# Attention, second block of each head pair: a vector-engine queue in another order

## The chip, the cores and the metric

The kernel runs on one core of one Trainium2 chip. The metric is the device time of one execution in microseconds (us). The engines are named as in the profile: PE is TensorE's matmul, DVE is VectorE, ACT is ScalarE, POOL is GpSimd, SP is SyncE, which here only issues DMAs.

## The reference

Three layers run one after the other. The change is in the first, attention in which a query sees the keys of its own hash bucket only (2 batches, 8 heads, 768 positions, 64 features a head):

```python
mask = q_bucket[:, :, :, None] == k_bucket[:, :, None, :]
scores = scale * np.matmul(q, k.transpose(0, 1, 3, 2))
scores = np.where(mask, scores, -1000000000.0)
scores = scores - np.max(scores, axis=-1, keepdims=True)
attn = np.exp(scores)
attn = attn / (np.sum(attn, axis=-1, keepdims=True) + 1e-09)
return np.matmul(attn, v).astype(np.float32)
```

Behind it stand a feed-forward layer (1536 tokens, 512 to 1024 to 512 features, with a softmax and a layer norm between) and a routed layer of 8 experts. The weights of the feed-forward layer arrive as float64 and are turned into float32 by bit operations, in small steps that the attention's program strews between its own.

## The kernel before, in words

Attention works on pairs of heads: j runs from 0 to 7, and the two heads of a pair lie side by side on the 128 partitions. The 768 queries of a pair are taken in two halves, i = 0 and i = 1. One pass for (j, i) is called a block here, written (j, 0) or (j, 1). In a block c runs over six chunks of 128 keys. `score` (L242) multiplies keys by queries on PE into one of three PSUM buffers called `ps`, ACT takes the exponential into SBUF (`pt`, L252), and POOL adds the exponentials up (`acc`, L256 for two chunks, L258 for the running sum). `rowmax` (L218) computes scores for a later block, into the same three buffers in turn, and DVE reduces them to the row maximum (L225, called a reduce below). So each `ps` buffer comes free either when ACT has taken the exponential or when DVE has reduced, and PE takes the buffers strictly in turn.

Work of the block before is put in at c = 1. In a block (j, 1) it is:

- `av(j, 0)` (L267): exponentials times values on PE, into `x`;
- `evac` (L272): DVE copies a column of `x` into `vb` (L276, the bias column), and ACT copies `x` to `xr` with that bias (L279);
- `sums`, which calls `total` (L281): PE sums the exponentials over keys into `pm` (L287), and DVE adds a small constant into `rb` (L293). In the last pair `direct` (L319) stands in its place: it goes on with a reciprocal (L324) and a product (L325) on DVE;
- `norm(j - 1)` (L313): DVE multiplies `xr` of the pair before by its quotients `rd`, which came back by DMA (L317, 128x768). The quotients come from `recip` (L302) in block (j, 0).

Each block also takes one unit of the float64 weights (`Weights.steps`, L414): `ops` is a list of five or six steps, and `some(m)` emits the next m of them. The steps are an ACT copy (L450), three DVE bit operations (L451, L454, L457, called first, second and last float64 step here), then for the first eight units an ACT cast (L466) and a POOL subtraction (L467), for the last eight an ACT scaling (L462). In a block (j, 1) the ACT copy stands at c = 0, the three DVE steps at c = 1, and the fourth of all (ACT) at c = 3. Units of the first kind fall to j = 0 to 3, of the second kind to j = 4 to 7.

There is no scheduler. Each engine executes its instructions in the order in which this Python code emits them, so the order of the calls in `run` is the order of every queue:

```python
self.av(j, 0, half[0])
some(3)
self.evac(j, 0)
(self.sums if nx else self.direct)(j, 0)
if j:
    self.norm(j - 1)
```

In the last block (7, 1) there are no row maxima left to compute, and `av(7, 1)` is split: its first three chunks are emitted at c = 4, the others behind the loop.

Of the kernel before, what the change touches and what calls it, by code (L numbers as in the profile page):

```python
# [118 lines left out]
class Attention:  # L119
# [207 lines left out]
    def run(self, n, extra, fills):  # L327
        self.last = (n - 1, 1)
        scan = [(j, i, c, kh) for j in range(n) for i in range(2) for c in range(3) for kh in range(2)]

        def scans(m):
            for x in scan[:m]:
                self.rowmax(*x)
            del scan[:m]

        next(extra)
        self.hash(0)
        self.tables()
        self.mask(0)
        scans(NC)  # L340
        self.submax(0, 0)
        scans(3)
        half = [tuple(range(NC)), (0, 1, 2), (3, 4, 5)]
        for j in range(n):
            nx = j + 1 < n
            for i in range(2):
                ops = next(extra, [])

                def some(m):
                    for f in ops[:m]:  # L350
                        f()
                    del ops[:m]

                for c in range(NC):
                    self.score(j, i, c)
                    scans(((2, 1, 0, 1, 1, 1), (2, 1, 1, 1, 1, 0))[i][c])
                    if c == 1:
                        if nx or i == 0:
                            self.submax(*((j, 1) if i == 0 else (j + 1, 0)))
                        if i == 0:  # L360
                            some(1)
                            if nx:
                                self.turn(j + 1)
                            some(1)
                            if j:
                                self.av(j - 1, 1, half[0])
                            if nx:
                                self.hash(j + 1)
                            if j:
                                self.evac(j - 1, 1)  # L370
                                self.sums(j - 1, 1)
                            some(1)
                            if nx:
                                self.mask(j + 1)
                                if j:
                                    self.load(j + 1, "v")
                            if j + 2 < n:
                                self.load(j + 2, "qk")
                        else:
                            self.av(j, 0, half[0])  # L380
                            some(3)
                            self.evac(j, 0)
                            (self.sums if nx else self.direct)(j, 0)
                            if j:
                                self.norm(j - 1)
                            if fills:
                                fills.pop(0)()
                    elif c != 2:
                        some(1)
                    if j and (i, c) == (0, 4):  # L390
                        self.recip(j - 1)
                    if c == 4 and (j, i) == self.last:
                        self.av(j, 1, half[1])
                some(9)
        self.av(n - 1, 1, half[2])
        self.evac(n - 1, 1)
        self.direct(n - 1, 1)
        for ops in extra:
            for f in ops:
                f()  # L400
# [821 lines left out]
```

## Time and profile before

| what | us |
|---|---|
| median of 3 runs (lowest, highest) | 637.66 (636.53, 638.45) |
| profiled execution, its own time | 638.34 |
| span of the profiled execution | 636.6 |
| PE busy in the span | 592.2 (93%) |
| DVE busy | 426.4 (67%) |
| ACT busy | 279.7 (44%) |
| POOL busy | 324.1 (51%) |

The span reaches from the first to the last instruction of the profile; the execution's own time is 1.74 us longer. The attention stage ends at some 262 us of the span. In the rows below each timeline line holds the start, the duration, the engine, the source line, the operation, out<-in with shapes, how many instructions are merged, and in brackets the idle time ahead of it on its engine with what ended that. Consecutive DVE instructions overlap a little in the records: the next starts up to 0.1 us before the end of the last.

### The profile page before, as it was taken

The numbers are of one execution on the slowest core, as the hardware profiler recorded it, in microseconds if no ns is written. First come the engines' busy times: TensorE is split into PE (matmuls) and PEld (weight loads), VectorE is DVE, ScalarE is ACT, GpSimd is POOL, SyncE is SP. The second block draws the span as 40 slices with busy tenths as digits, with TensorE's granted clock in tenths as the row PEclk, the third lists the DMA queues.
The fourth block names the chain that finished last, engine by engine and source line by source line (L and its number), as shares of the span: only waits on it lengthen the run. The fifth ranks groups of instructions, "written<-read, shape, count | busy, mean of one in ns | idle before, by whom it ended". The sixth has DMA issues, their size and how long they took to land.

```text
span 636.6 us, 10142 instructions
## 1 busy us (share of the span) xinstructions
PE 592.2 (93%) x3906; PEld 461.7 (73%) x3906; DVE 426.4 (67%) x800; ACT 279.7 (44%) x465; POOL 324.1 (51%) x262
## 2 busy tenths in 40 slices
PE   4889989899999998959999999989999999999994
PEld 2656556665666665648888888877998898899893
DVE  4868888787868786586767877764656636636630
ACT  3255454556575644343224233232734634544520
POOL 1148676666657577471100004031869659659641
PEclk9789999899999999989999999998999999999998
DMA  7134435362726241700000003016574674687200
GB/s 170 46 83 103 133 102 146 89 165 70 199 66 173 86 129 30 261 1 0 1 1 1 1 2 83 1 68 230 185 241 152 253 264 127 254 292 253 69 20 33
DMA packets 70165, 72.95 MB, mean 115 GB/s; under 512 B 36187, under 2 KB 47195, under 8 KB 70110
## 3 DMA queue, kind: packets, MB, share of 16 engines
q1 hardware_dynamic: 63838, 57.13, 30.1%
q10 hardware_dynamic: 4032, 8.79, 4.4%
q0 software_dynamic: 2240, 6.31, 2.9%
q8 instruction: 32, 0.52, 0.4%
q14 instruction: 23, 0.19, 0.1%
HBM read 58.39 MB, written 14.78 MB: 115 GB/s over the span
## 4 chain that ended last, share of the span: by engine, by line
PE 78%; DVE 12%; issue 3%; ACT 3%; DMA 2%; POOL 1%; SPq 0%; POOLq 0%; ACTq 0%; DVEq 0%
PE g L1004 14%; PE ps L214 14%; PE o L1026 14%; PE h L547 10%; PE y L547 10%; PE x L267 6%; DVE m L225 3%; DVE w L454 2%; PE ps L165 2%; PE t L610 2%; PE pm L287 1%; ACT pt L252 1%; PE x L971 1%; PE ps L200 1%; DVE w L457 1%
## 5 line engine op out<-in xcount | busy, mean ns | idle before, releaser
L256 POOL TENSOR_TENSOR acc<-pt,pt 128x768 f32<-128x768 f32 x48 | 92.3, 1923 | 98.6 <-ACT pt L252 98.6
L944 POOL TENSOR_TENSOR wl<-ws,wh 128x512 fp32r<-128x512 f32 x75 | 107.2, 1463 | 53.4 <-ACT wh L942 53.0
L225 DVE TENSOR_REDUCE m<-ps 128x2 f32<-128x768 f32 x96 | 89.1, 953 | 35.4 <-PE ps L214 34.6
L252 ACT ACTIVATE pt<-ps 128x768 f32<-128x768 f32 x96 | 76.2, 816 | 36.7 <-PE ps L214 36.1
L942 ACT CAST wh<-ws 128x512 fp32r<-128x512 f32 x128 | 70.3, 618 | 5.2 <-POOL wl L944 2.6
L267 PE MATMUL x<-pt,v 128*64 128x385 f32 x384 | 65.8, 491 | 0.0
L944 DVE TENSOR_TENSOR wl<-ws,wh 128x512 fp32r<-128x512 f32 x53 | 57.8, 1124 | 10.3 <-ACT wh L942 8.6
L1010 DVE SCALAR_TENSOR_TENSOR hl<-g,hh 128x512 fp32r<-128x512 f32 x32 | 22.1, 691 | 59.8 <-ACT hh L1009 49.3
L523 POOL TENSOR_TENSOR xl<-xT,xh 128x512 fp32r<-128x512 f32 x12 | 15.6, 1304 | 83.2 <-PE h L547 43.6
L258 POOL TENSOR_TENSOR acc<-acc 128x768 f32<-128x768 f32 x30 | 56.0, 1868 | 2.4
L1009 ACT ACTIVATE hh<-g 128x512 fp32r<-128x512 f32 x32 | 19.2, 599 | 81.4 <-PE g L1004 58.0
L547 PE MATMUL h<-wi,xh 128*128 128x512 f32 x192 | 51.2, 410 | 0.0
L1026 PE MATMUL o<-wh,hh 128*128 128x512 f32 x128 | 51.1, 399 | 0.0
L1026 PE MATMUL o<-wh,hl 128*128 128x512 f32 x128 | 50.5, 394 | 0.0
L1026 PE MATMUL o<-wl,hh 128*128 128x512 f32 x128 | 50.5, 394 | 0.0
L267 PEld LDWEIGHTS x<-pt,v 128*64 128x64 f32 x384 | 26.1, 137 | 31.7 <-issue 30.9
L214 PE MATMUL ps<-Hk,Hq 64*128 64x384 f32 x192 | 41.4, 421 | 7.3 <-ACT pt L252 7.2
L214 PE MATMUL ps<-Hq,Hk 64*128 64x384 f32 x192 | 39.5, 407 | 3.5 <-ACT pt L252 1.7
L547 PE MATMUL y<-wo,lh 128*128 128x512 f32 x176 | 42.6, 394 | 0.0
L547 PEld LDWEIGHTS h<-wi,xh 128*128 128x128 f32 x192 | 35.9, 194 | 8.0 <-ACT xh L538 0.6
L1004 PE MATMUL g<-xh,wh 128*128 128x256 f32 x256 | 41.3, 283 | 0.3 <-ACT xh L973 0.3
L1004 PE MATMUL g<-xl,wh 128*128 128x256 f32 x256 | 41.2, 282 | 0.0
(221 smaller groups left out, 1234.9 us busy)
## 6 DMA issues: line engine op xcount, KB each, us to landing
ws<-in_moe_w_dram SPq DMA_DIRECT2D x32, 1024.0 KB
scratch<-zero SPq DMA_DIRECT2D x7, 1030.0 KB
r<-scratch SPq DMA_DIRECT2D x16, 257.5 KB
raw<-in_moe_w_in_dram ACTq DMA_DIRECT2D x8, 512.0 KB
raw<-in_moe_w_out_dram ACTq DMA_DIRECT2D x8, 512.0 KB
q<-in_q_dram SPq DMA_DIRECT2D x16, 192.0 KB
v<-in_v_dram SPq DMA_DIRECT2D x16, 192.0 KB
k<-in_k_dram SPq DMA_DIRECT2D x14, 192.0 KB
```

Source lines behind the costliest of these rows:

```text
L214: self.nc.tensor.matmul(ps[:, h], w[r], x[r], start=(n == 0), stop=(n == len(jobs) - 1), tile_position=(D * h, 0))
L225: nc.vector.tensor_reduce(out=st["m", i][:, c, :, kh], in_=ps, axis=AX.X, op=ALU.max, negate=True)
L252: nc.scalar.activation(out=pt[:, :, 0:HW], in_=ps, func=AF.Exp, scale=0.125)
L256: nc.gpsimd.tensor_tensor(out=acc, in0=st["pt", i, c - 1][:, :, 0:HW], in1=pt[:, :, 0:HW], op=ALU.add)
L258: nc.gpsimd.tensor_tensor(out=acc, in0=parts.pop(), in1=acc, op=ALU.add)
L267: nc.tensor.matmul(st["x", i][D * h:D * h + D, 0:HW + 1], st["v"][:, h, c, :], st["pt", i, c][:, h, 0:HW + 1], start=(c == 0), stop=(c == ...
L547: nc.tensor.matmul(ps, a[:, k, :], w[j](k), start=(n == 0), stop=(n == len(jobs) - 1))
L942: nc.scalar.copy(hi[:, k, :], t[:, k, :])
L944: eng.tensor_tensor(out=lo[:, k, :], in0=t[:, k, :], in1=hi[:, k, :].bitcast(F32), op=ALU.subtract)
L1004: nc.tensor.matmul(ps[:, a, :], w[:, k, f * P:(f + 1) * P], x[:, k, :], start=(n == 0), stop=(n == 11))
L1010: nc.vector.scalar_tensor_tensor(out=hl[:, 2 * g:2 * g + 2, :], in0=ps, scalar=0.0, in1=hi.bitcast(F32), op0=ALU.max, op1=ALU.subtract)
L1026: nc.tensor.matmul(st["o"][t], h[:, f, t * P:(t + 1) * P], w[:, f % 4, :], start=(f == 0 and n == 0), stop=(f == 7 and n == 2),)
```

## The change

Only the branch for i = 1 changes. At c = 1 two of the three DVE float64 steps are emitted, then the bias column and the sums, and then the third step. The product `norm` leaves c = 1 and goes to c = 2, where no float64 step stands, behind that chunk's `score` and `rowmax`.

```diff
                         else:
                             self.av(j, 0, half[0])
-                            some(3)
+                            some(2)
                             self.evac(j, 0)
                             (self.sums if nx else self.direct)(j, 0)
-                            if j:
-                                self.norm(j - 1)
+                            some(1)
                             if fills:
                                 fills.pop(0)()
                     elif c != 2:
                         some(1)
+                    elif j and i:
+                        self.norm(j - 1)
```

The queues of PE, ACT, POOL and SP keep their order; only DVE's changes. On DVE, in block (2, 1), from the second float64 step on, before:

```order
L454 SCALAR_TENSOR_TENSOR w<-raw,w 128x512
L457 SCALAR_TENSOR_TENSOR w<-raw,w 128x512
L276 COPY vb<-x 128x1
L293 TENSOR_SCALAR rb<-pm 128x384
L317 TENSOR_TENSOR xT<-xr,rd 128x768
L225 TENSOR_REDUCE m<-ps 128x2 x6
```

and with the change (lines behind the edit are one number higher):

```order
L455 SCALAR_TENSOR_TENSOR w<-raw,w 128x512
L276 COPY vb<-x 128x1
L293 TENSOR_SCALAR rb<-pm 128x384
L458 SCALAR_TENSOR_TENSOR w<-raw,w 128x512
L225 TENSOR_REDUCE m<-ps 128x2
L317 TENSOR_TENSOR xT<-xr,rd 128x768
L225 TENSOR_REDUCE m<-ps 128x2 x5
```

The last float64 step (L457, now L458) has moved behind `vb` and `rb`, and the product L317 behind the first reduce. The blocks of the other pairs from 1 to 6 change in the same way; block (0, 1) has no product. In the last block (7, 1) DVE has, before:

```order
L454 SCALAR_TENSOR_TENSOR w<-raw,w 128x512
L457 SCALAR_TENSOR_TENSOR wo_70<-raw,w 128x512
L276 COPY vb<-x 128x1
L293 TENSOR_SCALAR rb<-pm 128x384
L324 RECIPROCAL rb<-rb 128x384
L325 TENSOR_TENSOR xT<-xr,rb 128x384
L317 TENSOR_TENSOR xT<-xr,rd 128x768
```

and with the change:

```order
L455 SCALAR_TENSOR_TENSOR w<-raw,w 128x512
L276 COPY vb<-x 128x1
L293 TENSOR_SCALAR rb<-pm 128x384
L324 RECIPROCAL rb<-rb 128x384
L325 TENSOR_TENSOR xT<-xr,rb 128x384
L458 SCALAR_TENSOR_TENSOR wo_70<-raw,w 128x512
L317 TENSOR_TENSOR xT<-xr,rd 128x768
```

Here the last float64 step moves behind the reciprocal and the product of `direct` as well.

## Rows read from the trace of the kernel before

**Rows 1.** Waits, whole span: who waited for whom, us in total, times, longest.

```profile
ACT xr L279 <- DVE vb L276: 51.3, 10, 6.3
```

**Rows 2.** Timeline of PE in block (3, 1), from the sums to the last score.

```profile
139.99 0.86 PE L287 MATMUL pm<-acc,ones 128*64 128x384 f32 x4
...
141.41 0.34 PE L214 MATMUL ps<-Fq,Fk 64*128 64x384 f32 x2
...
142.46 0.34 PE L214 MATMUL ps<-Fq,Fk 64*128 64x384 f32 x2
144.16 0.51 PE L214 MATMUL ps<-Hk,Hq 64*128 64x384 f32 x2 [1.36 <-ACT pt L252]
...
145.04 0.44 PE L214 MATMUL ps<-Hq,Hk 64*128 64x384 f32 x2 [0.19 <-DVE m L225]
...
146.20 0.34 PE L214 MATMUL ps<-Hq,Hk 64*128 64x384 f32 x2
```

**Rows 3.** Timeline of ACT and POOL in block (3, 1).

```profile
142.83 0.58 ACT L279 ACTIVATE xr<-x,vb 128x384 f32<-128x384 f32 x1 [6.20 <-DVE vb L276]
143.31 1.51 ACT L252 ACTIVATE pt<-ps 128x768 f32<-128x768 f32 x2
...
139.90 2.28 POOL L256 TENSOR_TENSOR acc<-pt,pt 128x768 f32<-128x768 f32 x1
144.89 1.84 POOL L256 TENSOR_TENSOR acc<-pt,pt 128x768 f32<-128x768 f32 x1 [2.72 <-ACT pt L252]
```

**Rows 4.** Timeline of DVE in block (3, 1).

```profile
138.30 2.18 DVE L454 SCALAR_TENSOR_TENSOR w<-raw,w 128x512 int32<-128x512 int32 x1
140.52 2.21 DVE L457 SCALAR_TENSOR_TENSOR w<-raw,w 128x512 int32<-128x512 int32 x1
142.65 0.14 DVE L276 COPY vb<-x 128x1 f32<-128x1 f32 x1
...
143.18 0.94 DVE L317 TENSOR_TENSOR xT<-xr,rd 128x768 f32<-128x768 f32 x1
144.04 1.81 DVE L225 TENSOR_REDUCE m<-ps 128x2 f32<-128x768 f32 x2
```

**Rows 5.** Timeline of POOL, DVE and PE in block (4, 1).

```profile
168.26 2.08 POOL L256 TENSOR_TENSOR acc<-pt,pt 128x768 f32<-128x768 f32 x1
168.69 2.20 DVE L454 SCALAR_TENSOR_TENSOR w<-raw,w 128x512 int32<-128x512 int32 x1
...
170.93 0.69 DVE L457 SCALAR_TENSOR_TENSOR wo<-raw,w 128x512 int32<-128x512 int32 x1
...
172.18 0.34 PE L214 MATMUL ps<-Fq,Fk 64*128 64x384 f32 x2
...
175.09 0.34 PE L214 MATMUL ps<-Hq,Hk 64*128 64x384 f32 x2
```

**Rows 6.** Timeline of DVE and PE in block (0, 1).

```profile
49.83 2.24 DVE L457 SCALAR_TENSOR_TENSOR w<-raw,w 128x512 int32<-128x512 int32 x1
...
51.77 0.34 PE L214 MATMUL ps<-Fq,Fk 64*128 64x384 f32 x2
...
55.24 0.44 PE L214 MATMUL ps<-Hq,Hk 64*128 64x384 f32 x2
```

**Rows 7.** Timeline of ACT, DVE and PE in the last block (7, 1).

```profile
255.47 0.72 ACT L462 ACTIVATE wo<-wo,g 128x512 f32<-128x512 f32 x1
...
256.38 1.52 DVE L325 TENSOR_TENSOR xT<-xr,rb 128x384 f32<-128x384 f32 x1
...
258.29 2.16 PE L267 MATMUL x<-pt,v 128*64 128x385 f32 x12
258.46 0.81 ACT L252 ACTIVATE pt<-ps 128x768 f32<-128x768 f32 x1 [1.56 <-PE ps L214]
```

**Rows 8.** Stretches: us, busy time of PE, PEld, DVE, ACT, POOL, granted clock, DMA.

```profile
110.00:113.90 3.90, 2.35 (x24) 1.76 (x20) 3.90 (x6) 2.19 (x4) 1.18 (x2) 1.00 0.85 230
113.90:117.40 3.50, 3.47 (x22) 3.48 (x24) 1.79 (x2) 1.11 (x2) 3.42 (x2) 0.54 0.23 48
```

## The prediction

> **What bounds the kernel now.** I read the waits first, then the timelines of PE, ACT, POOL and DVE for one block (j, 1), each against the others. PE sets the end of the attention stage, and its gaps in a block (j, 1) are made elsewhere. ACT's longest wait in this stage is that for the bias column `vb`: 51.3 us in ten waits [rows 1]. In block (3, 1) PE has done the score of chunk 3 at 142.80 (142.46 + 0.34) and then stands 1.36 us until 144.16, because the buffer that it wants next still holds chunk 2, whose score was done at 141.75 (141.41 + 0.34) [rows 2]. ACT takes that exponential only at 143.31, since `xr` is ahead of it in ACT's queue, and `xr` waited 6.20 us for `vb` [rows 3]. `vb` runs at 142.65, behind the last float64 step [rows 4]. A second wait follows: the score of chunk 4, at 145.04, waits for a reduce [rows 2], and that reduce stands at 144.04 behind `vb`, `rb` and the product L317 [rows 4]. So DVE's queue sets the pace for some 3 us in each block (j, 1), and the order of the queue is what changes.
>
> **How long the last float64 step takes.** It lasts 2.21 us in block (3, 1) [rows 4] and 0.69 in block (4, 1) [rows 5]. The difference is POOL. POOL's add ends at 142.18 (139.90 + 2.28) [rows 3], and the step ends at 142.73, 0.55 later [rows 4]. In block (4, 1) an add ends at 170.34 and the second float64 step at 170.89, again 0.55 later [rows 5]. A DVE operation with both inputs in SBUF waits there for the POOL instruction that is running and then runs nearly whole. The Trainium skill's page "SBUF — State Buffer", section "SBUF: two separate sides", says this as a rule: an exclusive lock on a shared port pair, held for the whole instruction by whichever began first. By proportional sharing a step would stretch with its overlap; by the rule an early start gains nothing, and these two ends agree with the rule.
>
> **Blocks (1, 1) to (3, 1).** I work out (3, 1) and take the other two as its repeats.
> - `vb` comes behind the second step, which ends at 140.48 (138.30 + 2.18) [rows 4]; that is 2.2 us earlier. `xr` then runs to about 141.2, and exponential 2 from 141.85, 0.1 after its score, for 0.81 [rows 7]. PE goes on at 142.76 in place of 144.16.
> - `rb` waits for PE's sums, done at 140.85 [rows 2], and with it the last step comes up at 141.4. POOL is in its add until 142.18, so the step still ends at 142.73. Moving it gains nothing in itself; it only lets `vb` and `rb` pass.
> - The first reduce now follows at 142.65, where `vb` stood, instead of 144.04: 0.53 for `vb` and `rb` and 0.86 for the product lie no longer ahead of it [rows 4]. PE's score of chunk 4 can start at 143.70 in place of 145.04.
> - The product comes next, at 143.52 (a reduce takes its place in the queue for 0.87), and the second reduce at 144.38, done at 145.33. PE would want that buffer at 144.76 (143.70 + 1.06, one chunk's score and row maximum: 142.46 − 141.41 [rows 2]) and gets it at 145.42. So a new wait of 0.66 us appears, for the reduce behind the product. Before, the last score started at 146.20 [rows 2]. The gain is 0.78 us a block, 2.34 in three.
>
> The product has two SBUF inputs too. POOL's next add follows exponential 3: score 3 ends at 142.80, the exponential at 143.71, the add starts at 143.78 (before, 0.07 after the exponential's end [rows 3]). The product at 143.52 is 0.26 us ahead of it. I take it that the product goes first and POOL waits; this is the narrowest step of the sum. If it goes first, POOL's add is still done earlier than before.
>
> **Blocks (4, 1) to (6, 1).** The second step ends at 170.89, POOL is idle from 170.34, so the last step takes 0.69 in either order [rows 5]. `vb` and `rb` end at 171.4, the step holds DVE until 171.94, the reduce, the product and the second reduce start at 171.94, 172.81 and 173.67, and the last is done at 174.63. The last score starts at 174.72 in place of 175.09 [rows 5]: 0.37 a block, 1.1 in three. POOL's add comes 0.98 after the end of score 3 (172.52), at 173.50, 0.7 behind the product's start.
>
> **Block (0, 1)** has no product. The last step ends at 52.07 as before [rows 6]; the reduce starts at 51.99 and ends at 52.93; the score of chunk 4 starts at 53.03 and the last at 54.09, in place of 55.24 [rows 6]: 1.15 us.
>
> **Block (7, 1) loses.** The last step now stands behind the product of `direct`, which ends at 257.90 (256.38 + 1.52), so it ends at 258.50. ACT's scaling L462 needs it. It ran at 255.47 and now runs at 258.5, and exponentials 4 and 5 stand behind it in ACT's queue. Exponential 5 started at 258.46 [rows 7]; with 0.62 for the scaling's place in the queue (0.72 less an overlap of 0.1) and 0.70 for exponential 4's (1.51 − 0.81 [rows 3, 7]) it now starts at 259.8 and ends at 260.6. PE's second part of `av`, which ended at 260.45 [rows 7], needs 0.7 for the last chunk after that (a third of 2.16) and ends at 261.4, and the feed-forward layer starts that much later: 1.0 us lost. `norm(6)` itself is wanted much later.
>
> **Sum.** 1.15 + 2.34 + 1.1 − 1.0 = 3.6 us gained. Against the profiled execution of 638.34 that is 634.7. That execution lies 0.7 above the median of 637.66; from the median it is **634.1**. The bounds of the one unknown place: the product costs 0.86 where it stands, or, behind a POOL add, 2.9 (below).
>
> **The rivals.**
> - *POOL goes first (slower).* If the add takes the port before the product in (1, 1) to (3, 1), the product waits until 145.62 (143.78 + 1.84) and needs 0.8 more, to 146.42; the second reduce ends at 147.29, and the last score starts at 147.4, 1.2 later than before. Three blocks lose 3.5, the others still gain 1.15 + 1.1 − 1.0: +2.3, so 640.0 from the median. The product of `direct` shows such a wait: 128x384 in 1.52 us [rows 7]. It decides at a lead of 0.26 us, which must shrink to nothing; three blocks have the same lead, so they would go together. The Trainium skill's page "Perfetto Trace Analysis", section "GPSIMD Engine Instruction", speaks for this rival: recorded spans of that engine are to be treated as unreliable. By that the add's true start could be before the recorded one; no run here shows it. Chance 0.14.
> - *The gain is given back.* PE runs ahead, but POOL's chain of adds starts only some 0.5 earlier and the next blocks wait for something that did not move. Against it: the sums of (j, 1) are taken a whole stretch of PE work later. Then only (0, 1) and (7, 1) count, 1.15 − 1.0, about 637.5. Chance 0.20.
> - *The clock comes back too.* Right behind the gap of block (2, 1) the granted clock is 0.54 for 3.50 us, after 2.35 of 3.90 us busy [rows 8]; that is mostly 1.2 instead of 2.4 GHz and costs 1.6 us (3.50 × 0.46). PE's waits in such a block shrink and split. If the clock stays at 2.4 GHz there, the time is 632.5. Chance 0.15.
>
> **How the numbers follow.** The forecast itself gets 0.51. What a measurement can tell from no change is about 0.3%, 1.9 us, so the line for faster is 635.8. Forecast and clock rival lie below it: 0.66. The second rival is the same: 0.20. The first is slower: 0.14. The range leaves out the first rival alone and takes in the clock rival and the second: 631.8 to 637.8.
>
> **What would show it.** Right: `xr` waits about 2 us less for `vb` in blocks (0, 1) to (3, 1); PE's 1.36 us wait for the exponential is gone and one of about 0.7 for the reduce behind the product is there; the last step still ends 0.55 behind POOL's add in (0, 1) to (3, 1); the product lasts 0.94; in (7, 1) L462 waits for the float64 step and the feed-forward layer starts 1.0 late. Wrong: a product of 2 us or more, blocks after (j, 1) that take back the gain, or a last block that loses nothing.

## The result, and the profile after

| | before | changed |
|---|---|---|
| median of seven runs each, us | 637.66 | 632.62 |
| ratio of the times | 1 | 0.9911, 95% interval 0.989 to 0.9932 |
| profiled execution, its own time | 638.34 | 631.40 |
| its span | 636.6 | 629.7 |

By the medians the change makes the kernel 5.0 us faster, by the ratio 5.7 (4.3 to 7.0). One of the seven runs of the changed kernel was slow, 1975.9 us, and is left out of the ratio. Forecast were 3.6, with 5.2 for the case that the clock comes back too. Where the time came from is read block by block. I take the start of PE's sums of (j, 0) (L287, in the middle of block (j, 1)) and the next transposes (L165, at the start of work for the next pair) from the timelines of PE. Pair 6 has no transposes behind it, so sums to sums stands there, and for pair 7 sums of (7, 0) to sums of (7, 1):

| stretch | before | changed | gain | forecast |
|---|---|---|---|---|
| (0, 1) | 9.88 | 8.88 | 1.00 | 1.15 |
| (1, 1) | 10.46 | 9.35 | 1.11 | 0.78 |
| (2, 1) | 11.60 | 9.35 | 2.25 | 0.78 |
| (3, 1) | 10.23 | 9.33 | 0.90 | 0.78 |
| (4, 1) | 9.37 | 8.90 | 0.47 | 0.37 |
| (5, 1) | 9.39 | 8.90 | 0.49 | 0.37 |
| (6, 1) | 13.30 | 12.81 | 0.49 | 0.37 |
| (7, 1) | 8.07 | 9.20 | −1.13 | −1.0 |
| sum | | | 5.6 | 3.6 |

Block (3, 1) as an example. Before, it begins at 139.99 [rows 2] and ends at this row:

```profile
150.22 0.87 PE L165 MATMUL ps<-ident,q 128*128 128x128 f32 x6
```

Changed, it lies between these two:

```profile
134.77 0.87 PE L287 MATMUL pm<-acc,ones 128*64 128x384 f32 x4
...
144.10 0.87 PE L165 MATMUL ps<-ident,q 128*128 128x128 f32 x6
```

All stretches between these, from transposes or sums to the next sums, agree within 0.02 us in the two traces. The spans differ by 6.9: 5.6 here, 0.9 ahead of the first sums, where the edit changes nothing, and 0.5 behind the attention stage. I take these last 1.3 for what one execution differs from another: in the nine traces of this record the first sums begin between 46.80 and 49.70 us.

The waits of the changed kernel, whole span, the row that answers to [rows 1]:

```profile
ACT xr L279 <- DVE vb L276: 38.1, 10, 4.6
```

51.3 has become 38.1, and the longest single wait 4.6 instead of 6.3. In blocks (0, 1) to (3, 1) each wait is 3.9 to 4.0 us where it was 6.2 to 6.3. PE, ACT, POOL and DVE in block (3, 1) of the changed kernel; take 5.22 off the times of [rows 2 to 4], since the sums of this block begin at 134.77 instead of 139.99:

```profile
134.67 2.28 POOL L256 TENSOR_TENSOR acc<-pt,pt 128x768 f32<-128x768 f32 x1
...
135.36 0.58 ACT L279 ACTIVATE xr<-x,vb 128x384 f32<-128x384 f32 x1 [3.97 <-DVE vb L276]
...
135.68 0.56 DVE L293 TENSOR_SCALAR rb<-pm 128x384 f32<-128x384 f32 x1 [0.35 <-PE pm L287]
...
136.16 1.35 DVE L458 SCALAR_TENSOR_TENSOR w<-raw,w 128x512 int32<-128x512 int32 x1
...
136.65 0.81 ACT L252 ACTIVATE pt<-ps 128x768 f32<-128x768 f32 x1 [0.70 <-PE ps L214]
...
137.43 0.94 DVE L225 TENSOR_REDUCE m<-ps 128x2 f32<-128x768 f32 x1
137.52 0.51 PE L214 MATMUL ps<-Hk,Hq 64*128 64x384 f32 x2
...
138.30 0.94 DVE L317 TENSOR_TENSOR xT<-xr,rd 128x768 f32<-128x768 f32 x1
...
138.43 0.44 PE L214 MATMUL ps<-Hq,Hk 64*128 64x384 f32 x2 [0.23 <-DVE m L225]
138.59 2.33 POOL L256 TENSOR_TENSOR acc<-pt,pt 128x768 f32<-128x768 f32 x1 [1.64 <-ACT pt L252]
...
139.16 1.81 DVE L225 TENSOR_REDUCE m<-ps 128x2 f32<-128x768 f32 x2
...
140.16 0.44 PE L214 MATMUL ps<-Hq,Hk 64*128 64x384 f32 x2 [0.41 <-DVE m L225]
```

PE's 1.36 us for the exponential are gone: it goes on at 137.52 with no idle time beside the row. Two waits for reduces stand there, 0.23 for score 4, which had 0.19 before [rows 2], and a new one of 0.41 for the last score. The last float64 step (L458) ends at 137.51, 0.56 behind POOL's add, which ends at 136.95. The product starts 0.29 ahead of POOL's next add (0.25 to 0.30 in the three blocks) and lasts 0.94; that add takes 2.33 instead of 1.84 [rows 3], so here it is POOL that waits.

The last block of the changed kernel, DVE, ACT and PE, against [rows 7]:

```profile
248.82 1.54 DVE L325 TENSOR_TENSOR xT<-xr,rb 128x384 f32<-128x384 f32 x1
...
250.28 0.68 DVE L458 SCALAR_TENSOR_TENSOR wo<-raw,w 128x512 int32<-128x512 int32 x1
...
250.99 0.72 ACT L463 ACTIVATE wo<-wo,g 128x512 f32<-128x512 f32 x1 [2.94 <-DVE wo L458]
251.62 1.49 ACT L252 ACTIVATE pt<-ps 128x768 f32<-128x768 f32 x2
252.46 1.57 PE L267 MATMUL x<-pt,v 128*64 128x385 f32 x8 [0.84 <-ACT pt L252]
```

ACT's scaling waits 2.94 us for the float64 step, and PE waits 0.84 for the exponentials behind it.

### The profile page after: what moved, and what is told of

It is laid out like the page before. It is cut to its first block, busy times and chain, and to the rows that moved or that the text cites. A ratio compares the mean times of both kernels' runs of the same rounds, so it can differ in the third digit from the quotient of the medians.

```text
span 629.7 us, 10138 instructions
## 1 busy us (share of the span) xinstructions
PE 590.2 (94%) x3906; PEld 459.1 (73%) x3906; DVE 420.9 (67%) x800; ACT 280.9 (45%) x465; POOL 325.5 (52%) x262
## 4 chain that ended last, share of the span: by engine, by line
PE 79%; DVE 11%; ACT 3%; issue 3%; DMA 2%; POOL 1%; SPq 0%; POOLq 0%; ACTq 0%; DVEq 0%
PE g L1005 15%; PE o L1027 14%; PE ps L214 13%; PE h L548 10%; PE y L548 10%; PE x L267 7%; DVE m L225 3%; PE ps L165 2%; PE t L611 2%; PE pm L287 2%; DVE w L455 1%; ACT pt L252 1%; PE ps L188 1%; PE x L972 1%; PE ps L200 1%
```

## The experiments

Theory: in a block (j, 1) PE restarts when DVE's queue lets it, so each part is worth what it takes from in front of `vb` or of a reduce; the product is cheap only as long as it starts before POOL's add. Rivals: one of the two parts brings everything; the engines share and don't wait; the tail hangs on POOL. Beside the first four kernels the kernel before took 638.84, beside the last three 638.35, so the times below are to be compared by their ratios. The block lengths decide: between traces in which the order is the same they repeat within a few hundredths, but for block (0, 1), which takes 8.85 to 8.89 in five traces with the moved step, 8.38 in that of the run on the last block and 8.73 in that of the product one chunk later. In these two POOL's add starts 0.67 and 0.25 ahead of the sums instead of 0.09 or 0.10, so the last step behind it waits less.

**The float64 step alone.** The product goes back to c = 1:

```diff
                             some(1)
+                            if j:
+                                self.norm(j - 1)
                             if fills:
                                 fills.pop(0)()
...
-                    elif j and i:
-                        self.norm(j - 1)
```

> Only the float64 step moves behind vb and rb; the product stays at c = 1, between the step and the first reduce. My theory (DVE's order sets PE's restart, and each part is worth what it takes from in front of a reduce or of vb): blocks (1,1) to (3,1) gain 0.5 to 0.65 us each, because vb frees ACT two us earlier and the reduce starts 0.53 earlier but still behind the product; blocks (4,1) to (6,1) gain 0.1 to 0.2 each; (0,1) keeps its 1.0; (7,1) keeps its loss of 1.1. Sum about 2.4 us against the kernel before, 635.2 (633.8 if the slow clock behind block (2,1) goes as well). Rival (the step's own move brings everything, the product's place nothing): all of the 5.0, 632.6.

Measured 636.15, ratio 0.9959 (0.9943 to 0.9976). (0, 1) takes 8.89, (1, 1) to (3, 1) 9.70, 9.80 and 9.71, (7, 1) 9.19. Against 10.23, the length before of an undisturbed block of the first kind, that is 0.5 a block, the forecast's lower end. Of the second kind (5, 1) takes 9.25 and (6, 1) 13.17, 0.14 each. Only (4, 1) got longer, 9.91. DVE and PE in that block:

```profile
168.46 0.96 DVE L317 TENSOR_TENSOR xT<-xr,rd 128x768 f32<-128x768 f32 x1 [0.55 <-DMA rd<-rd]
...
170.34 0.44 PE L214 MATMUL ps<-Hq,Hk 64*128 64x384 f32 x2 [1.35 <-DVE m L225]
```

So early in DVE's queue the product waits 0.55 us for the DMA that brings its quotients, and the reduce behind it comes late by that much, so that PE waits 1.35. I had not foreseen this wait. In (5, 1) and (6, 1) of the same trace the product comes as early and does not wait, so how often it happens stays open; in both traces of the changed kernel, which puts the product a reduce later, it is not there. The step alone brings 2.6 us by the ratio, so it does not bring everything.

**The product alone.** All three steps stay ahead of `vb`:

```diff
-                            some(2)
+                            some(3)
                             self.evac(j, 0)
                             (self.sums if nx else self.direct)(j, 0)
-                            some(1)
```

> Only the product moves behind the first reduce; all three float64 steps stay ahead of vb, as in the kernel before. My theory: PE's 1.36 us wait for exponential 2 stays in blocks (1,1) to (3,1), since vb is as late as before; the wait for the reduce behind the product's old place goes, worth about 0.3 us in each of the six blocks with a product; (0,1) gains nothing and (7,1) loses nothing, its order is that of before. Sum about 1.7 us, 636.0. Rival (the product's move brings everything): 632.6.

Measured 634.33, ratio 0.9936 (0.9912 to 0.996), some 4.1 us: more than the 1.7 expected. By blocks: (0, 1) 9.87 and (7, 1) 8.07, nothing gained or lost, as expected; (1, 1) to (3, 1) 9.88, 9.90, 9.88, that is 0.35 off 10.23; (4, 1) to (6, 1) 9.02, 8.99, 12.92, that is 0.35 to 0.40. Six such gains are 2.2, and 0.23 comes from (1, 1), whose length before holds a wait of its own (below): 2.4. Block (2, 1) gains 1.35 more since it has no slow clock in this trace. The interval of the times, 2.6 to 5.6 us, fits 3.8 and just misses 2.4.

Where no other wait comes in, the two parts add up: 0.52 and 0.35 in (3, 1) make 0.87, both together gave 0.90; 0.14 and 0.40 in (5, 1) make 0.54, together 0.49. In (4, 1) they don't, because of the DMA in the first run: it lost 0.54 there, the product alone gained 0.35, and both together gained 0.47.

**The last block in its old order.**

```diff
-                            some(2)
+                            some(2 if nx else 3)
                             self.evac(j, 0)
                             (self.sums if nx else self.direct)(j, 0)
-                            some(1)
+                            some(1 if nx else 0)
```

> The changed kernel, but the last block (7,1) keeps the order of before: all three float64 steps ahead of vb. My theory: the 1.1 us that the last block loses come back, since the ACT scaling no longer waits for a step behind the product of the last pair: 631.5, and the sums of (7,1) end 19.4 us after those of (7,0) began, as before, in place of 20.6. Rival (the tail is set by POOL's adds, which move as well): no change, 632.6.

Measured 631.76, ratio 0.9894 (0.9868 to 0.992). The times alone can't tell that from the changed kernel, the trace can: sums to sums 8.10, where before has 8.07 and the changed kernel 9.20. The loss of the last block is the step behind `direct` and nothing else. Another 0.5 us of this trace's gain is the (0, 1) named above, which the edit does not touch.

**The product late by half a microsecond.** A reduce over 384 columns, whose result nobody uses, stands ahead of the product:

```diff
                     elif j and i:
+                        pad = self.sp.tile([P, 1], F32, tag="pad", name="pad")
+                        self.nc.vector.tensor_reduce(out=pad, in_=self.st[j - 1]["xr"][:, 0], axis=AX.X, op=ALU.max)
                         self.norm(j - 1)
```

> The changed kernel with one more DVE operation of about 0.5 us (a reduce over 384 columns whose result nobody uses) right ahead of the product, so that the product comes after the start of POOL's add in blocks (1,1) to (3,1) instead of 0.29 us before it, and still before it in (4,1) to (6,1). Theory of the lock (the DVE operation waits until POOL's add is done): in (1,1) to (3,1) the product lasts some 2.2 to 2.5 us in place of 0.94 and the last score of the block comes about 1.9 us later; in (4,1) to (6,1) it lasts 0.94 and costs the 0.5 us alone: about 7 us slower than the changed kernel, 639.8. Theory without a lock (the two engines share): the product stretches by at most 0.5, and the whole costs 0.5 to 1 us a block in all six: 636 to 638.

Measured 641.68, ratio 1.0046 (1.002 to 1.0071): slower than the kernel before. Block (3, 1) of this kernel, DVE, POOL and PE:

```profile
146.23 0.54 DVE L391 TENSOR_REDUCE pad<-xr 128x1 f32<-128x384 f32 x1
...
146.51 1.85 POOL L256 TENSOR_TENSOR acc<-pt,pt 128x768 f32<-128x768 f32 x1 [1.62 <-ACT pt L252]
146.69 2.48 DVE L317 TENSOR_TENSOR xT<-xr,rd 128x768 f32<-128x768 f32 x1
148.44 2.41 POOL L258 TENSOR_TENSOR acc<-acc 128x768 f32<-128x768 f32 x1
149.10 1.81 DVE L225 TENSOR_REDUCE m<-ps 128x2 f32<-128x768 f32 x2
...
150.09 0.44 PE L214 MATMUL ps<-Hq,Hk 64*128 64x384 f32 x2 [2.39 <-DVE m L225]
```

Now the add starts 0.18 ahead of the product. The product lasts 2.48 and ends at 149.17, 0.81 behind the add's end at 148.36. PE waits 2.39 for the reduce behind it. The block takes 11.33 instead of 9.33, 2.0 more for half a microsecond of delay. In (4, 1) to (6, 1), where the product still starts 0.19 to 0.25 ahead of the add, it keeps 0.94 and the blocks take 9.36, 9.33 and 13.28, half a microsecond more. That is the lock of the first rival, with its price of some 2 us. By sharing it would have stretched by at most 0.5. Blocks (1, 1) and (2, 1) take 13.43 and 12.71: the slow clock comes on top, and in (1, 1) a scaling of `g` of 1.28 us; so the kernel is some 9 us above the changed one by the two ratios, where 7 were expected. Two stretches of this kernel, the first inside block (1, 1), the second over the end of (2, 1), with the columns of [rows 8]; the granted clock is 0.75 and 0.83:

```profile
78.00:90.00 12.00, 9.35 (x72) 8.06 (x70) 10.05 (x12) 5.71 (x8) 9.57 (x6) 0.75 0.65 164
...
118.00:128.00 10.00, 9.82 (x70) 7.33 (x72) 7.23 (x8) 5.90 (x8) 7.31 (x5) 0.83 0.17 54
```

**The product in the next pair's first half.** This goes on from the run on the last block. `norm` leaves (j, 1) altogether, but for the last pair:

```diff
                             some(1)
+                            if j > 1:
+                                self.norm(j - 2)
                             if nx:
                                 self.mask(j + 1)
...
-                    elif j and i:
+                    elif i and not nx:
                         self.norm(j - 1)
```

> The changed kernel with the last block's old order (as in the run on the last block) and with the product moved once more: norm(j - 1) goes from block (j,1) to block (j+1,0), behind its last float64 step, where DVE stands idle for 1.6 us and POOL is idle as well; only norm(6) stays in (7,1). My theory (the second reduce of a block (j,1) waits for the product that stands ahead of it): PE's 0.4 us wait for that reduce goes in the six blocks, and (j+1,0) grows by nothing. From the sums of (j,0) to the next transposes (1,1) to (3,1) take 8.9 us as (0,1) does, in place of 9.35, and (4,1) to (6,1) 8.5 in place of 8.9. Sum 2.5 us below the run on the last block, 3.6 below the changed kernel: 629.0. Rival (the product costs DVE 0.87 wherever it stands, or PE then waits for an exponential at the same time): no more than the last block's 1.1, 631.5.

Measured 628.27, ratio 0.9841 (0.9823 to 0.9858): the fastest of all, and the interval is clear of that of the changed kernel on the same occasion. (2, 1) and (3, 1) take 8.86 and 8.83, as (0, 1) with 8.85; (4, 1) and (5, 1) 8.40 and 8.39; (7, 1) 8.07. DVE in block (3, 0), where the product now stands, and then DVE and PE in block (3, 1):

```profile
120.75 0.68 DVE L460 SCALAR_TENSOR_TENSOR w<-raw,w 128x512 int32<-128x512 int32 x1
121.35 0.95 DVE L317 TENSOR_TENSOR xT<-xr,rd 128x768 f32<-128x768 f32 x1
123.04 0.96 DVE L225 TENSOR_REDUCE m<-ps 128x2 f32<-128x768 f32 x1 [0.74 <-PE ps L214]
...
135.26 1.81 DVE L225 TENSOR_REDUCE m<-ps 128x2 f32<-128x768 f32 x2
...
137.42 0.34 PE L214 MATMUL ps<-Hq,Hk 64*128 64x384 f32 x2
```

The product takes part of an idle stretch of 1.6 us and leaves 0.74 of it; the stretches from transposes to the next sums stay as they were, but for the last one, up to the sums of (7, 0), which is 0.2 longer. In (3, 1) the two reduces follow each other, and PE's last score has no idle time beside its row. Block (1, 1) alone does not gain, 9.37: there DVE's small scaling of the vector `g` runs into POOL's add, from 81.07 to 82.90, and lasts as long:

```profile
81.26 1.67 DVE L430 TENSOR_SCALAR g<-g 128x8 f32<-128x8 f32 x1
```

**The product one chunk later.**

```diff
-                    elif j and i:
+                    if j and (i, c) == (1, 3):
                         self.norm(j - 1)
```

> The changed kernel with the product one chunk later, at c = 3, behind the second reduce. Theory of the lock: POOL's add has begun by then in (1,1) to (3,1), so the product waits for its end and lasts about 2.1 us; the third reduce comes at 141.1 of the changed kernel's time scale in place of 140.0, and PE waits there about 1.2 us, so a block is 0.5 us longer than in the changed kernel; (4,1) to (6,1) likewise or less: 634 to 636. Rival (one reduce more ahead of the product frees PE earlier, and the third reduce has slack): faster than the changed kernel by 0.4 a block, 630.

Measured 637.31, ratio 0.9975 (0.9957 to 0.9993), worse than I expected. (1, 1) to (3, 1) take 10.0 (0.5 more than the changed kernel expected, 0.67 measured), and (4, 1) to (6, 1) 9.96, 9.95 and 13.66, 0.85 to 1.06 more, where I expected no more than in the first three. PE, DVE and POOL in block (3, 1):

```profile
141.03 1.85 POOL L256 TENSOR_TENSOR acc<-pt,pt 128x768 f32<-128x768 f32 x1 [1.63 <-ACT pt L252]
...
141.61 2.08 DVE L317 TENSOR_TENSOR xT<-xr,rd 128x768 f32<-128x768 f32 x1
...
143.62 0.94 DVE L225 TENSOR_REDUCE m<-ps 128x2 f32<-128x768 f32 x1
...
144.62 0.51 PE L214 MATMUL ps<-Hk,Hq 64*128 64x384 f32 x2 [0.83 <-DVE m L225]
```

The product waits for the add as the lock says, 2.08 us, and the reduce behind it holds PE for 0.83. What I missed, as I read it, is that the late reduce then also delays the next ones; I did not test that apart. Block (7, 1), which the expectation does not mention, takes 9.85 where the changed kernel has 9.20. Here the product of `direct` starts 0.09 ahead of POOL's add, does not wait, and the float64 step behind it waits in its place, which sends ACT's scaling on late:

```profile
254.91 0.56 DVE L325 TENSOR_TENSOR xT<-xr,rb 128x384 f32<-128x384 f32 x1
255.00 2.14 POOL L256 TENSOR_TENSOR acc<-pt,pt 128x768 f32<-128x768 f32 x1 [2.52 <-ACT pt L252]
255.39 2.30 DVE L458 SCALAR_TENSOR_TENSOR wo<-raw,w 128x512 int32<-128x512 int32 x1
```

**The changed kernel again.**

> The changed kernel itself, to have it on the same chip and beside the same runs of the kernel before as the two others: 0.9911 of the kernel before, 632 to 633. If the slow clock of block (2,1) in the first trace of before was chance, the blocks (1,1) to (3,1) read 9.35 us here as in its first profile.

Measured 632.70, ratio 0.9902 (0.9885 to 0.992). The stretches are 8.87, 9.33, 9.34, 9.32, 8.92, 8.87, 12.77 and 9.20, within 0.04 of its first trace.

## Why the prediction was right, point by point

- *DVE's order sets PE's restart.* Shown: each part alone moves the blocks by its own share, and the shares add up in (3, 1) and (5, 1), where no other wait comes in.
- *The last float64 step still ends behind POOL's add.* Right: 0.56 behind it in (3, 1), 0.55 forecast. The move gains by what it lets pass.
- *The product comes to the port first.* Right, and as narrow as said: a lead of 0.29 measured, 0.26 forecast. The late product showed the other side, 0.18 behind the add, at 2.0 us a block, 1.2 + 0.78 forecast; its last score, at 150.09, is 147.38 on the time scale of [rows 2], 147.4 forecast. So the rival was a real one; it did not happen. On the warning that recorded spans of GpSimd are unreliable (the Trainium skill, "Perfetto Trace Analysis", section "GPSIMD Engine Instruction"): here the order of the recorded starts did tell who waited, in both directions, at 0.2 to 0.3 us.
- *Blocks (1, 1) to (3, 1), 0.78 each.* Undersized: (3, 1) gained 0.90. I let PE follow 0.1 after each reduce; it follows after 0.06 (138.37 to 138.43, 140.10 to 140.16), and the stretch behind the last score is 0.08 shorter too. The new wait of 0.66 was reckoned from the start of one score to the start of the next; so reckoned it is 0.67 (140.16 less 138.43 + 1.06), while the row's 0.41 counts from the recorded end of the matmul ahead, 139.75. The 0.23 ahead of score 4 is in the forecast too, as its start at 143.70 (143.65 measured), but was not named as a wait.
- *A term left out.* (1, 1) gains 0.2 more than (3, 1). DVE's scaling of `g` (128x8) took 1.39 us in that block before, where it ended 0.03 behind a POOL add, and takes 0.15 in the changed kernel, where it starts as the add ends. The sum did not price it. The two rows, before and changed:

```profile
86.17 1.39 DVE L427 TENSOR_SCALAR g<-g 128x8 f32<-128x8 f32 x1
```

```profile
83.12 0.15 DVE L428 TENSOR_SCALAR g<-g 128x8 f32<-128x8 f32 x1
```

- *Blocks (4, 1) to (6, 1), 0.37 each.* 0.47 to 0.49: in (4, 1) the last score comes within 0.02 of the forecast, and the stretch behind it is 0.08 shorter, as above. *(0, 1), 1.15:* 1.00; its last score comes 0.07 later than forecast, and the stretch behind it is 0.08 longer.
- *The last block loses 1.0.* Right: 1.13, and undoing that one step gave it back.
- *The clock rival.* It came in the profile: (2, 1) gains 2.25, of which 1.35 are what the slow clock had added to its length before, against 1.6 forecast. The changed kernel has the full clock in the whole block:

```profile
105.88:115.23 9.35, 8.63 (x78) 6.63 (x76) 7.67 (x10) 5.91 (x9) 7.68 (x5) 1.00 0.69 191
```

In the traces of the runs on either part alone, too, no such block has the slow clock; in that of the late product, with longer gaps, two have. Of the kernel before there is one trace only, so in how many of its runs it loses the clock is not shown, nor how much of the 5.0 is the clock's; without it the traces give 4.2. That the median came out near the 5.2 of this rival is no proof of it: the blocks gained 0.6 more than forecast, and the share of the clock stays open.
- *The gain is given back later.* It was not: the stretches between the blocks stayed equal.

## What to carry to other kernels

Where two engines hand buffers to a third in turn, look at what stands ahead of the instruction that frees the buffer, and move all that nobody waits for behind it, or better to a stretch where its engine is idle anyway: here that was worth twice as much as one place back in the queue (block (3, 1): 9.71 with the step alone moved, 9.33 with the product a reduce later, 8.83 with it in the next pair). Look in the trace for operations of one shape with two durations; on DVE they marked a wait for POOL here, and a few tenths of a microsecond decided between a hidden operation and two microseconds. An order that helps seven blocks should be looked at again in the last one, where other work waits for the step that was put back.

## What the runs showed of the hardware

A DVE operation that reads two SBUF tensors ended 0.55 us (512 columns) or 0.81 (768 columns) after the end of the POOL add that ran when it came, in every block in which it was held up. If it came 0.29 ahead, POOL's add lasted 2.33 instead of 1.84; a lead of 0.09 was enough in one block. A scaling of 128x8 took 0.15, 1.39 and 1.67 us in three kernels, depending on the add that it met, and ended 0.03 behind the add in the two long cases; that an operation so small is held up as long I had not expected.
